# A fused linear-attention and two-MLP kernel: 14 low parts by TensorE and ScalarE, the reciprocals in place, and the last second layers later

## The chip, the cores and the metric

The kernel runs on one core of one Trainium2 chip. The metric is the device time of one execution in microseconds (us), taken as the median of three runs. A profile is one further execution under the hardware profiler; its times count from the first instruction.

## The reference, cut to what matters

Inputs are q, k, v and a decay alpha of shape (4 batches, 8 heads, 768 steps, 48), and weights for two MLPs.

```
state = alpha[t] * state + k[t] v[t]^T          # per batch and head, D = 48
y[t]  = q[t] . state                            # -> x: (3072 tokens, 384)
x1    = elu(x @ w_in) @ w_out                   # hidden 2048
out   = sum over 4 experts e of p[e] * (relu(x1 @ w1[e]) @ w2[e])    # hidden 1024 each
```

## The kernel before

**Attention.** The 768 steps are cut into 6 chunks of 128; a unit is one chunk of one batch (24 units). Within a unit P is the running product of the decay. Scaled by P, q and k turn the recurrence into matrix products: q becomes q*P and k becomes k/P. `prep0` makes P with a VectorE scan and has ScalarE make the reciprocal rP as exp(-ln P). `prep1` (its inner `newton`) refines it on VectorE: t = P*rP, k = k*rP, k = (2 - t)*k. `prep2` makes q = q*P. Then come `scores`, `ktrans` (transposes k through a bank of PSUM), `yout_t` and `state`.

**First MLP.** The float32 operands are split into a high part rounded to float32r and a low part, the rest; a product is three matmuls (high-high, high-low, low-high). An item is one chunk (512 tokens over the 4 batches) with one block of 128 hidden units: 6 x 16 = 96 items. `first` (through `g1`, L422) makes h in a bank of PSUM with 9 matmuls; `elu` is two ScalarE operations (L431, L432) and one VectorE operation in PSUM (L433, the `unit`); `parts` (L438, L439) has ScalarE copy h to the high part g[:,0] and VectorE subtract that from h to give the low part g[:,1]; `second` (through `g2a`, L447) takes both parts two iterations later in 9 matmuls.

**Order.** During this loop TensorE, ScalarE, VectorE and GpSimd each execute strictly in the order in which the code emits their instructions. `self.later` puts an operation into a queue that the next `flush` emits; there are two flushes in an iteration. Each iteration also has two slots, (i, 0) and (i, 1), which carry the steps of the attention units of the next chunk and, in the first 12 iterations, the conversion of the remaining first-MLP weights (`conv_f64`: one ScalarE scaling L406, three VectorE bit operations L77 to L83, then a ScalarE high copy L375 and a VectorE low part L376). The first 14 items (`WIDE`) are "late": the unit is the last thing emitted in the iteration, and the two parts are made in the next one.

**Banks.** `first` and `ktrans` draw their banks from the same ring of three (h0, h1, h2) in turn. A bank is free again when its low part has been made. In chunk 0, `ktrans` falls in slots (0, 0), (3, 0), (6, 1) and (9, 1); after each of them the next two `first` calls are given the bank of the item two before, where otherwise it is that of the item three before.

**Second MLP.** Three rounds of 11 groups; each group has 15 steps (11 in the last one of a round). A step is 3 matmuls (L726) into a bank, then VectorE operations that combine it with running sums (S0 to S5), some on GpSimd. The second-layer matmuls (L773) of the group before are spread between the steps in proportion to a weight per step, `cum`, built from the count of VectorE operations. In group 0 there is no group before; there the second layers of the last two first-MLP items, in six pieces of 3 matmuls (L447), stand between the steps. From group 1 on the ring has two banks.

Of the kernel before, what the change touches and what calls it, by code (L numbers as in the profile page):

```python
# [8 lines left out]
F32 = mybir.dt.float32  # L9
# [78 lines left out]
class _Fast:  # L88
# [50 lines left out]
    def consts(self):  # L139
        nc, const = self.nc, self.const  # L140
        self.zero = self.big.tile([128, 512], mybir.dt.bfloat16, tag="X1", name="zero")
        nc.vector.memset(self.zero, 0.0)
        self.plo = const.tile([128, 1], F32, name="plo")
        nc.vector.memset(self.plo, P_LO)
        self.ident = const.tile([128, 128], F32, name="ident")
        make_identity(nc, self.ident)
        self.mask = const.tile([128, 128], mybir.dt.bfloat16, name="mask")
        nc.gpsimd.memset(self.mask, 1.0)
        nc.gpsimd.affine_select(
            out=self.mask, in_=self.mask, compare_op=ALU.is_ge, fill=0.0,  # L150
            base=0, pattern=[[1, 128]], channel_multiplier=-1,
        )
        self.pacc = const.tile([128, 2 * NCH * B], F32, name="pacc")
        nc.vector.memset(self.pacc, 0.0)
        self.st = []
        for b in range(B):
            s = self.ap.tile([128, NP, 64], F32, tag=f"st{b}", name=f"st{b}")
            nc.vector.memset(s, 0.0)
            self.st.append(s)

    def warm(self, n):
        if n:
# [35 lines left out]
    def prep0(self, u):  # L198


        nc = self.nc
        raw = self.raw[u]
        Pf = self.ap.tile([128, NP * (C + 2)], F32, tag="P", name="P", bufs=3)
        P = Pf.rearrange("p (a t) -> p a t", a=NP)[:, :, 2:C + 2]
        rP = self.ap.tile([128, NP, C], F32, tag="rP", name="rP", bufs=3)
        nc.vector.tensor_tensor_scan(
            Pf, raw[:, A0:V0], self.plo.to_broadcast([128, V0 - A0]), 1.0, ALU.mult, ALU.max
        )
        n = 2 * (u[0] * B + u[1])
        l = self.ap.tile([128, NP, C], F32, tag="rP", name="lnP", bufs=3)  # L210

        def inverse():
            nc.scalar.activation(out=l, in_=P, func=AF.Ln)
            nc.scalar.activation(out=rP, in_=l, func=AF.Exp, scale=-1.0, accum_out=self.pacc[:, n:n + 1])
            nc.scalar.activation(out=l, in_=l, func=AF.Exp, accum_out=self.pacc[:, n + 1:n + 2])

        self.later(inverse)
        self.P[u], self.rP[u] = P, rP

    def prep1(self, u):  # L220

        nc = self.nc
        raw, P, rP = self.raw[u], self.P[u], self.rP.pop(u)
        k = raw[:, K0:A0].rearrange("p (a t) -> p a t", a=NP)

        def newton():
            t = self.ap.tile([128, NP, C], F32, tag="rP", name="nt", bufs=3)
            nc.vector.tensor_tensor(out=t, in0=P, in1=rP, op=ALU.mult)
            nc.vector.tensor_tensor(out=k, in0=k, in1=rP, op=ALU.mult)
            nc.vector.scalar_tensor_tensor(  # L230
                out=k, in0=t, scalar=2.0, in1=k, op0=ALU.subtract, op1=ALU.mult, reverse0=True
            )

        self.later(newton)

    def prep2(self, u):
        nc = self.nc
        raw, P = self.raw[u], self.P[u]
        q = raw[:, Q0:K0].rearrange("p (a t) -> p a t", a=NP)
        nc.vector.tensor_tensor(out=q, in0=q, in1=P, op=ALU.mult)  # L240

    def scores(self, u):

# [134 lines left out]
    def unit_steps(self, u, nxt):  # L378
# [4 lines left out]
        s.append(N(self.prep1))  # L383
        s.append([(self.xtrans, ((u[0], u[1] - 1),))] if u[1] else [])
        s.append([(self.yout_t, (u,))] + ([] if last else [(self.state, (u,))]))
        s.append(N(self.prep2))
        return s


# [431 lines left out]
    def run(self):  # L821
# [26 lines left out]
        def prep(u):  # L848
            self.prep0(u)
            self.prep1(u)  # L850
            self.prep2(u)

        pe_order = tc.manual_schedule(engines={mybir.EngineType.PE})
        pe_order.__enter__()
# [101 lines left out]
        order.__enter__()  # L956
        self.queue = []

        gone = None
        for i in range(n1):  # L960
            h, late = first(items[i]), i < WIDE
            if gone:
                gs[items[i - 1]], low = self.parts(gone)
            self.flush()
            for s in slots.pop((i, 0), []):
                do(s)
            if gone:
                low()
                gone = None
            unit = self.elu(h)  # L970
            if not late:
                unit()
            self.flush()
            if i >= LA:
                second(items[i - LA])
            for s in slots.pop((i, 1), []):
                do(s)
            for f, a in post.pop(i, []):
                f(*a)
            if late:  # L980
                unit()
                gone = h
            else:
                gs[items[i]], low = self.parts(h)
                self.queue.insert(0, low)
# [7 lines left out]
        for i in range(ng + 1):  # L993
# [2 lines left out]
            if i:  # L996
                self.hb = ("h0", "h1")
            if i == 0:
                first_work = {1 + 2 * n: (it, k) for n, (it, k) in enumerate((it, k) for it in items[-LA:] for k in range(KD))}
            elif i > 0:  # L1000
                work = self.layer2(i - 1, G.pop(i - 1))
            if i == ng:
# [23 lines left out]
                    for j in range(1, 5):  # L1026
                        put((2, 5, 8, 9)[j - 1], self.load_xc, r + 1, j)

            dve = [sum(1 for o in ops if "b" in o[2:]) for _, ops in (STEPS if q < NG - 1 else STEPS2)]
            cum = [0]  # L1030
            for n in range(steps):
                cum.append(cum[-1] + 1 + dve[n] + (dve[n - 1] if n else 0))
# [198 lines left out]
```

## Time and profile before

| | |
|---|---|
| median of 3 runs | 1266.61 us (1266.56 to 1269.72) |
| profiled execution: its own time | 1271.87 us |
| its span, first to last instruction | 1270.1 us |
| TensorE matmul busy | 1244.1 us (98%) |
| VectorE, ScalarE, GpSimd busy | 891.5, 588.6, 484.8 us |
| mean granted TensorE clock | 0.990 of full speed |

Busy times are of the profiled execution. Matmuls are pipelined, so a busy TensorE is not necessarily one at its peak. A group's mean duration is longer than the distance between two starts of such instructions in a row, because successive ones overlap.

### The profile page before, as it was taken

What the parts mean: (1) busy time and instruction counts of PE and PEld (TensorE: products, weight loads), DVE (VectorE), ACT (ScalarE), POOL (GpSimd) and SP (SyncE); (2) the same over time, 40 slices, a digit from 0 to 9 for tenths busy, and PEclk for the clock granted to TensorE, in tenths of its full rate; (3) what the DMA queues carried; (4) which work ended last, traced back from release to release, by engine and by line L of the source; (5) the groups of instructions that cost most, each with busy time, mean ns of one, the idle gap of its engine ahead of it and who ended that gap; (6) DMA issues with size and microseconds to landing.
All of it is one profiled execution on the core that took longest, in us unless ns stands there. A gap on an engine that the chain in (4) does not pass through costs nothing.

```text
span 1270.1 us, 17591 instructions
## 1 busy us (share of the span) xinstructions
PE 1244.1 (98%) x6457; PEld 1013.5 (80%) x6457; DVE 891.5 (70%) x1465; ACT 588.6 (46%) x1076; POOL 484.8 (38%) x378
## 2 busy tenths in 40 slices
PE   8899999999999999999999999999999999999997
PEld 5677888888888788878888887888888878888886
DVE  7999677777777758766666756675767575766664
ACT  5666566666656667544343423333343324233241
POOL 0000000000000000066778856777878475356562
PEclk8799999999999999999999999999999999999999
DMA  6564346464756455835464477855456774435231
GB/s 232 180 218 156 105 151 229 178 214 167 251 187 224 159 193 211 281 124 215 160 238 167 170 284 285 304 191 218 164 204 236 276 266 169 158 135 181 100 124 66
DMA packets 71535, 246.80 MB, mean 194 GB/s; under 512 B 6680, under 2 KB 38264, under 8 KB 62096
## 3 DMA queue, kind: packets, MB, share of 16 engines
q1 hardware_dynamic: 70576, 240.87, 53.6%
q10 hardware_dynamic: 864, 4.72, 0.9%
q8 instruction: 53, 0.87, 0.3%
q14 instruction: 42, 0.34, 0.1%
HBM read 182.21 MB, written 63.36 MB: 193 GB/s over the span
## 4 chain that ended last, share of the span: by engine, by line
PE 88%; DVE 7%; issue 2%; ACT 1%; POOL 1%; DMA 0%; DVEq 0%; POOLq 0%; ACTq 0%
PE h L726 25%; PE t L773 14%; PE t L447 14%; PE h L422 13%; PE a L773 10%; PE h L773 5%; PE a L250 1%; PE a L307 1%; PE a L314 1%; DVE cv L80 1%; DVE cv L83 1%; PE h L271 1%; PE a L341 1%; DVE w_W L376 1%; DVE sm L258 1%
## 5 line engine op out<-in xcount | busy, mean ns | idle before, releaser
L704 POOL TENSOR_TENSOR g_W<-c,g_W 128x512 fp32r<-128x512 f32 x128 | 164.5, 1300 | 677.6 <-DVE u L746 538.8
L746 DVE TENSOR_TENSOR u<-h,u 128x512 f32<-128x512 f32 x258 | 177.6, 688 | 86.5 <-PE h L726 85.6
L422 PE MATMUL h<-x,w_W 128*128 128x512 f32 x864 | 218.4, 397 | 8.3 <-DVE g L439 8.2
L726 PE MATMUL h<-xc_Q,wa 128*128 128x512 f32 x780 | 219.0, 390 | 2.7 <-DVE c L746 2.0
L447 PE MATMUL t<-g,w_W 128*128 128x512 f32 x864 | 215.1, 392 | 0.3 <-DVE g L439 0.3
L701 ACT ACTIVATE g_W<-c 128x512 fp32r<-128x512 f32 x128 | 80.2, 627 | 270.1 <-DVE c L746 153.5
L422 PEld LDWEIGHTS h<-x,w_W 128*128 128x128 f32 x864 | 162.3, 190 | 44.8 <-DVE g L439 9.7
L447 PEld LDWEIGHTS t<-g,w_W 128*128 128x128 f32 x864 | 160.9, 188 | 34.6 <-DVE g L439 0.7
L726 PEld LDWEIGHTS h<-xc_Q,wa 128*128 128x128 f32 x780 | 146.0, 188 | 34.8 <-DVE c L746 2.5
L773 PE MATMUL t<-g_W,wb 128*128 128x512 f32 x576 | 157.6, 389 | 0.0
L773 PEld LDWEIGHTS t<-g_W,wb 128*128 128x128 f32 x576 | 108.1, 188 | 22.6
L702 ACT ACTIVATE c<-c 128x512 f32<-128x512 f32 x192 | 121.5, 633 | 7.3
L433 DVE SCALAR_TENSOR_TENSOR h<-e,h 128x512 f32<-128x512 f32 x96 | 66.6, 693 | 73.9 <-ACT e L432 73.8
L746 DVE TENSOR_TENSOR c<-u,h 128x512 f32<-128x512 f32 x123 | 84.1, 686 | 47.4 <-PE h L726 42.7
L740 DVE COPY u<-h 128x512 f32<-128x512 f32 x99 | 67.9, 690 | 64.1 <-PE h L726 62.7
L726 PE MATMUL h<-xc_W,wa 128*128 128x512 f32 x390 | 109.8, 390 | 0.7 <-DVE c L746 0.7
L704 POOL TENSOR_TENSOR g_X<-c,g_X 128x512 fp32r<-128x512 f32 x64 | 82.0, 1297 | 69.3 <-ACT c L702 65.9
L773 PE MATMUL a<-g_W,wb 128*128 128x512 f32 x384 | 108.2, 389 | 0.0
L701 ACT ACTIVATE g_X<-c 128x512 fp32r<-128x512 f32 x64 | 40.1, 627 | 132.0 <-DVE c L746 73.2
L726 PEld LDWEIGHTS h<-xc_W,wa 128*128 128x128 f32 x390 | 72.9, 188 | 17.3 <-DVE c L746 1.6
L431 ACT ACTIVATE e<-h 128x512 f32<-128x512 f32 x96 | 57.3, 597 | 60.8 <-PE h L422 59.4
L439 DVE TENSOR_TENSOR g<-h,g 128x512 fp32r<-128x512 f32 x96 | 65.8, 686 | 26.8 <-ACT g L438 26.5
(138 smaller groups left out, 1861.0 us busy)
## 6 DMA issues: line engine op xcount, KB each, us to landing
wa<-wad SPq DMA_DIRECT2D x33, 1536.0 KB, 6.5
wb<-wbd SPq DMA_DIRECT2D x30, 1536.0 KB, 7.2
raw<-in_att_dram SPq DMA_DIRECT2D x22, 964.0 KB, 5.2
wad<-wh SPq DMA_DIRECT2D x44, 384.0 KB, 2.9
wbd<-wh SPq DMA_DIRECT2D x43, 384.0 KB, 3.7
xcd<-xh SPq DMA_DIRECT2D x30, 512.0 KB, 2.9
wraw<-in_wm_dram SPq DMA_DIRECT2D x16, 768.0 KB, 4.3
wraw<-in_we_dram SPq DMA_DIRECT2D x20, 576.0 KB, 4.7
```

The lines of the kernel that those rows point to most:

```text
L422: nc.tensor.matmul(h[:, 0:n], w[:, wl, fi, k * 128:(k + 1) * 128], x[:, xl, k, n0:n0 + n], start=(k == 0 and i == 0), stop=(k == KD - 1 an ...
L431: nc.scalar.activation(out=e, in_=h, func=AF.Relu, scale=-1.0)
L433: return lambda: nc.vector.scalar_tensor_tensor(out=h, in0=e, scalar=-1.0, in1=h, op0=ALU.add, op1=ALU.max)
L439: return g, lambda: nc.vector.tensor_tensor(out=g[:, 1], in0=h, in1=g[:, 0].bitcast(F32), op=ALU.subtract)
L447: nc.tensor.matmul(self.xa[k][:, 0:n], w[:, wl, fi, DM + k * 128:DM + (k + 1) * 128], g[:, gl, 0:n], start=(first and i == 0), stop=(last ...
L701: nc.scalar.activation(out=g[:, n, 0], in_=v, func=AF.Relu)
L702: nc.scalar.activation(out=v, in_=v, func=AF.Relu)
L704: lambda: nc.gpsimd.tensor_tensor(out=g[:, n, 1], in0=v, in1=g[:, n, 0].bitcast(F32), op=ALU.subtract)
L726: nc.tensor.matmul(b, w[:, wl], x[:, xl], start=(j == 0), stop=(j == 2))
L740: nc.vector.tensor_copy(out, b)
L746: (nc.vector if "b" in (a0, a1) or dst == "S5" else nc.gpsimd).tensor_tensor(out=out, in0=val(a0, b), in1=val(a1, b), op=ALU.add if op == ...
L773: nc.tensor.matmul(oa[m, d], wt[:, f, wl, d * 128:(d + 1) * 128], G[m][:, f, gl], start=first, stop=last)
```

## The change

1. For the first 14 items the VectorE subtraction L439 goes. In its place TensorE adds -1 times the high part to h in its bank (one matmul with a new tile `minus`, minus the identity), emitted after `second`, and ScalarE copies the bank to g[:,1], emitted after slot (i, 1) and what follows it.
2. rP is written over the decay values in the unit's raw tile. `newton` now multiplies q and rP by P in one VectorE operation of 2 x 512 columns; `prep2` goes, and with it the separate tile for rP and t.
3. The six pieces of the last two second layers in group 0 move from after steps 1, 3, 5, 7, 9, 11 to after steps 4, 7, 9, 11, 13, 14.
4. The weight of a step counts the VectorE operation on S5 that reads no bank (one, in step 7 of every group but the last of a round).

```diff
+        self.minus = self.ap.tile([128, 128], F32R, tag="minus", name="minus")
+        nc.scalar.mul(self.minus, self.ident, -1.0)
...
-        rP = self.ap.tile([128, NP, C], F32, tag="rP", name="rP", bufs=3)
+        rP = raw[:, A0:A0 + NP * C].rearrange("p (a t) -> p a t", a=NP)
...
-        l = self.ap.tile([128, NP, C], F32, tag="rP", name="lnP", bufs=3)
+        l = self.ap.tile([128, NP, C], F32, tag="lnP", name="lnP", bufs=2)
...
         def newton():
-            t = self.ap.tile([128, NP, C], F32, tag="rP", name="nt", bufs=3)
-            nc.vector.tensor_tensor(out=t, in0=P, in1=rP, op=ALU.mult)
             nc.vector.tensor_tensor(out=k, in0=k, in1=rP, op=ALU.mult)
+            qr = raw[:, 0:3 * NP * C].rearrange("p (x a t) -> p x a t", x=3, a=NP)[:, 0:3:2]
+            nc.vector.tensor_tensor(
+                out=qr, in0=qr, in1=P.unsqueeze(1).to_broadcast([128, 2, NP, C]), op=ALU.mult
+            )
             nc.vector.scalar_tensor_tensor(
-                out=k, in0=t, scalar=2.0, in1=k, op0=ALU.subtract, op1=ALU.mult, reverse0=True
+                out=k, in0=rP, scalar=2.0, in1=k, op0=ALU.subtract, op1=ALU.mult, reverse0=True
             )
...
-        s.append(N(self.prep2))
+        s.append([])
...
             if gone:
-                gs[items[i - 1]], low = self.parts(gone)
+                g, _ = self.parts(gone)
+                gs[items[i - 1]] = g
             self.flush()
             for s in slots.pop((i, 0), []):
                 do(s)
-            if gone:
-                low()
-                gone = None
             unit = self.elu(h)
...
             if i >= LA:
                 second(items[i - LA])
+            if gone:
+                nc.tensor.matmul(gone, self.minus, g[:, 0], start=False, stop=True, skip_group_check=True)
             for s in slots.pop((i, 1), []):
                 do(s)
             for f, a in post.pop(i, []):
                 f(*a)
+            if gone:
+                nc.scalar.copy(g[:, 1], gone)
+                gone = None
             if late:
                 unit()
                 gone = h
...
-                first_work = {1 + 2 * n: (it, k) for n, (it, k) in enumerate((it, k) for it in items[-LA:] for k in range(KD))}
+                pieces = [(it, k) for it in items[-LA:] for k in range(KD)]
+                first_work = dict(zip((4, 7, 9, 11, 13, 14), pieces))
...
-            dve = [sum(1 for o in ops if "b" in o[2:]) for _, ops in (STEPS if q < NG - 1 else STEPS2)]
+            dve = [sum(1 for o in ops if "b" in o[2:] or o[1] == "S5") for _, ops in (STEPS if q < NG - 1 else STEPS2)]
```

## Rows read from the trace of the kernel before

**Rows 1.** The page: busy tenths and granted TensorE clock, 40 slices of 31.75 us

```profile
DVE  7999677777777758766666756675767575766664
...
PEclk8799999999999999999999999999999999999999
```

**Rows 2.** Stages by window: start:end, length, then busy us (instructions) per engine, clock

```profile
44.00:127.69 83.69, 74.63 (x500) 58.72 (x499) 80.62 (x117) 54.90 (x95) 0.00 (x0) 0.94 0.56 187
127.69:532.08 404.39, 404.31 (x2495) 330.26 (x2496) 296.81 (x574) 257.29 (x520) 0.00 (x0) 1.00 0.57 196
```

**Rows 3.** Waits of TensorE, 40 to 135 us: total, times, longest

```profile
PE h L422 <- DVE g L439: 8.2, 3, 4.2
PE a L250 <- ACT cv L406: 0.5, 1, 0.5
```

**Rows 4.** Timeline of TensorE, first layer: start, length, instruction [idle before]

```profile
54.70 4.21 PE L422 MATMUL h<-x,w_W 128*128 128x512 f32 x9 [4.19 <-DVE g L439]
...
63.91 2.20 PE L422 MATMUL h<-x,w_W 128*128 128x512 f32 x9
...
69.68 2.20 PE L422 MATMUL h<-x,w_W 128*128 128x512 f32 x9
...
73.78 2.33 PE L422 MATMUL h<-x,w_W 128*128 128x512 f32 x9
...
86.49 2.33 PE L422 MATMUL h<-x,w_W 128*128 128x512 f32 x9
...
93.34 3.79 PE L422 MATMUL h<-x,w_W 128*128 128x512 f32 x9 [2.47 <-DVE g L439]
...
113.94 2.33 PE L422 MATMUL h<-x,w_W 128*128 128x512 f32 x9 [1.54 <-DVE g L439]
...
120.73 2.34 PE L422 MATMUL h<-x,w_W 128*128 128x512 f32 x9
...
133.72 2.20 PE L422 MATMUL h<-x,w_W 128*128 128x512 f32 x9
```

**Rows 5.** Timeline of VectorE in iterations 1 and 2

```profile
53.96 0.68 DVE L439 TENSOR_TENSOR g<-h,g 128x512 fp32r<-128x512 f32 x1
54.56 0.68 DVE L228 TENSOR_TENSOR nt<-P,rP 128x512 f32<-128x512 f32 x1
...
61.88 0.35 DVE L351 TENSOR_TENSOR tmp<-a,st 128x192 f32<-128x192 f32 x1
```

**Rows 6.** Timeline of ScalarE: iterations 1, 4 and 7

```profile
56.03 0.92 ACT L406 ACTIVATE cv<-wraw 128x768 f32<-128x768 f32 x1
...
70.72 0.59 ACT L438 CAST g<-h 128x512 fp32r<-128x512 f32 x1 [1.51 <-DVE h L433]
...
75.93 0.50 ACT L375 CAST x<-xr 128x384 fp32r<-128x384 f32 x1
...
92.73 0.63 ACT L213 ACTIVATE lnP<-P 128x512 f32<-128x512 f32 x1 [1.82 <-DVE P L206]
...
94.78 0.89 ACT L406 ACTIVATE cv<-wraw 128x768 f32<-128x768 f32 x1
```

**Rows 7.** Groups by line and shape: busy us, mean ns, idle before

```profile
L439 DVE TENSOR_TENSOR g<-h,g 128x512 fp32r<-128x512 f32 x96 | 65.8, 686 | 26.8 <-ACT g L438 26.5
...
L438 ACT CAST g<-h 128x512 fp32r<-128x512 f32 x96 | 56.2, 586 | 47.8 <-DVE h L433 47.3
...
L376 DVE TENSOR_TENSOR w_W<-cv,w_W 128x768 fp32r<-128x768 f32 x16 | 15.2, 950 | 0.0
```

**Rows 8.** Timelines of TensorE and VectorE where group 0 ends

```profile
548.56 0.96 PE L726 MATMUL h<-xc_Q,wa 128*128 128x512 f32 x3 [2.04 <-DVE c L746]
...
547.81 0.69 DVE L746 TENSOR_TENSOR c<-u,h 128x512 f32<-128x512 f32 x1
```

**Rows 9.** Waits of TensorE, 566 to 1260 us

```profile
PE h L726 <- DVE c L746: 0.7, 2, 0.4
PE h L726 <- DVE u L746: 0.7, 2, 0.4
```

More of the change, by code (lines that the diff above doesn't have):

```diff
@@ L226, in newton @@
         def newton():
-            t = self.ap.tile([128, NP, C], F32, tag="rP", name="nt", bufs=3)
-            nc.vector.tensor_tensor(out=t, in0=P, in1=rP, op=ALU.mult)
             nc.vector.tensor_tensor(out=k, in0=k, in1=rP, op=ALU.mult)
+            qr = raw[:, 0:3 * NP * C].rearrange("p (x a t) -> p x a t", x=3, a=NP)[:, 0:3:2]
+            nc.vector.tensor_tensor(
+                out=qr, in0=qr, in1=P.unsqueeze(1).to_broadcast([128, 2, NP, C]), op=ALU.mult
+            )
             nc.vector.scalar_tensor_tensor(
-                out=k, in0=t, scalar=2.0, in1=k, op0=ALU.subtract, op1=ALU.mult, reverse0=True
+                out=k, in0=rP, scalar=2.0, in1=k, op0=ALU.subtract, op1=ALU.mult, reverse0=True
             )
         self.later(newton)
[L236 to L240, printed above, removed]
     def scores(self, u):
@@ L850, in prep @@
             self.prep1(u)
-            self.prep2(u)
         pe_order = tc.manual_schedule(engines={mybir.EngineType.PE})
```

## The prediction

> **What bounds the kernel now.** The tenths of the page come first: VectorE stands at 9 from the second to the fourth slice and the granted clock is below full there; later neither holds [rows 1]. The windows put edges to it. From 44.0 us, where the first item starts, to 127.7 us VectorE is busy 80.6 of 83.7 us and TensorE 74.6; from 127.7 to 532.1 us TensorE is busy 404.3 of 404.4 at full clock [rows 2]. So whatever the change does to the attention steps or to the first layer after 127.7 us is worth nothing unless it shortens TensorE, and it doesn't. The question is when TensorE reaches the steady stage: `first(15)`, the first-layer matmuls of item 15, at 133.72 us [rows 4]. The waits then name the limit before that: 8.2 us in three waits of `first` for the VectorE low part g [rows 3], at items 2, 8 and 11 [rows 4]. These are just places where `ktrans` has taken a bank of the ring, so that `first(i)` is given the bank of item i-2: the wait is for a bank, and a bank is free when its low part is made.
>
> **1, the low parts: what goes.** VectorE loses 14 operations. One lasts 0.686 us [rows 7], but the next starts 0.60 us after it [rows 5], so 14 x 0.60 = 8.4 us go from an engine that is nearly full.
>
> **What is added.** TensorE gets 14 matmuls of 512 columns; nine last 2.20 us [rows 4], so 0.24 each, 3.4 us. ScalarE gets 14 copies like L438, 0.59 us [rows 7], 8.3 us on an engine busy 54.9 of 83.7 [rows 2]; in sum that hurts nobody.
>
> **Where the bank is freed.** Here I choose against the sum of loads. Before, VectorE made the low part in mid-iteration. Now the bank needs: high part (ScalarE), then all of `second`, the negative matmul, then whatever ScalarE has before the copy, which is emitted last. All engines keep their order, so I step through the bank's seven gates (`first` of items 2, 4, 5, 7, 8, 10, 11), and take each stretch between gates from the old rows plus 0.24 us for each negative matmul in it. Seven is found from the ring: after each `ktrans` the next two `first` take the bank of item i-2.
>
> *Item 2.* In iteration 1 ScalarE runs the weight scaling L406 at 56.03 us for 0.92 [rows 6]; the low copy comes behind it. With 0.1 us of overlap it ends at 56.85 + 0.59 = 57.44, and `first(2)` starts at 57.5 instead of 54.70 [rows 4]: +2.8. Before, the low part was made at 53.96 [rows 5]. VectorE cannot use its free time: its decay operation needs `state`, which TensorE issues after `first(2)`; it ran at 61.88 [rows 5], and moves with it.
>
> *Items 3, 4.* 63.91 - 54.70 = 9.21 us from `first(2)` to `first(3)`, half clock included [rows 4], plus 0.24: 66.95 (+3.0). To `first(4)` 5.77 plus 0.24, and now a gate: matmul tail and two handovers (0.25, estimated from the 0.06 between the end of the low part and a waiting `first`, twice or so, and a tail) and the copy, 0.59: 73.8 against 69.68, +4.1.
>
> *Item 5.* The low copy of item 2 also stands ahead of item 3's high part on ScalarE, which so moves from 70.72 to about 73.55. From there to the end of the x cast before, 75.93 + 0.50, ScalarE had 5.7 us of work [rows 6]: weights, the logarithm and two exponentials, elu, L406, x. Behind that comes the copy of item 3: 73.55 + 5.7 + 0.5 = 79.8, so `first(5)` moves from 73.78 to 79.8, +6.0.
>
> *Item 7.* 86.49 - 73.78 = 12.71 without an idle TensorE, plus 0.48: 93.0, +6.5. Its own gate is covered by `scores` and `ktrans`, which follow the negative matmul; the same for item 10.
>
> *Item 8.* ScalarE in iteration 7: 2.2 us for `first(7)`, 1.2 for elu, then logarithm and exponentials, 94.78 - 92.73 = 2.05 [rows 6], L406 0.8, copy and handover 0.65: 93.0 + 6.9 = 99.9 against 93.34, +6.5. TensorE has ended `second(5)` and the negative matmul at about 97.45 and idles 2.45 us.
>
> *To the end.* From `first(8)` to `first(12)` it was 120.73 - 93.34 = 27.39 us; less 1.6 of slow clock, 1.54 and 0.45 of idle time [rows 3, 4], plus four negative matmuls (0.96) and 2.4 us of idle at item 11, where the order is that of item 8: 27.2, so 127.1 (+6.4). Three more matmuls (0.7) against the 0.6 us that TensorE loses there now: `first(15)` at 140.2, +6.4 to 6.5. I take +6.4.
>
> **The clock.** After 4.19 and 2.47 us idle the nine matmuls took 4.21 and 3.79 us, half clock for most of them; after 1.54 us idle 2.33 us, full clock [rows 4]. The new idles at items 8 and 11 (2.4 us) are nearest to the one that fell, yet a little shorter: bounds 0 and 2 x 1.6 us. I take one of the two: +1.5.
>
> **A rule that bears on it.** In iteration 7 the L406 at 94.78 needs only weights, yet it runs behind a logarithm that waited 1.82 us for VectorE [rows 6]: ScalarE didn't overtake. The Trainium skill, "PSUM — Partial Sum Buffer", section on engine and sequencer instructions, says the queues of ScalarE, VectorE and GpSimd are strict FIFO; by that rule, with which the trace agrees, the copy waits for the logarithm and the sum stands; if ScalarE could overtake, the copy of item 6 would end some 2 us sooner.
>
> **2, the reciprocals.** `newton` before: three operations of 0.60, plus q 0.60. After: 0.60 + 0.60, and one of 1,024 columns. From 512 to 768 columns the length grows from 0.686 to 0.950 us [rows 7], 1.03 ns a column, so its start-to-start time is 0.60 + 512 x 1.03 ns = 1.13. It saves 0.07 us for each of 24 units, four of which lie in the VectorE stage: 0.3 us, which the gates above swallow. In the prelude it costs or gives 0.6 at most: q*P used to run while VectorE waited for the first exponential, and now comes after it. I take 0 with bounds -0.6 and +0.6. `minus` is one 128-column ScalarE operation under 0.59 us while ScalarE has nothing to do: 0; if it stands ahead of the first logarithm, that is in the 0.6.
>
> **3, the last second layers.** At the end of group 0 TensorE waits 2.04 us for the last VectorE operation, 547.81 + 0.69 [rows 8]. Steps 12 to 14 now have two pieces (2 x 0.68) among them, but steps 0 to 4 are bare: VectorE's seven operations there (4.2 us) outlast five steps of 0.68 us, and step 4 waits about 0.6 for its bank. The same VectorE work, with less waiting in it, ends near 547.7: -0.75, bounds -1.4 and +0.5. The three copies of x1 and their DMA, on ScalarE's queue, move behind the last activations of the group; the banks they free are wanted 10 us later, and the data a round later.
>
> **4, the weights.** TensorE waits 0.7 us behind u and 0.7 behind c in all of the second MLP [rows 9]. More matmuls behind the S5 operation can take the first: -0.7, bounds -1.4 and +0.5 (another step is left shorter).
>
> **The sum.** +6.4 + 1.5 - 0.75 - 0.7 = +6.45 us. The profiled execution took 1271.87 us (span 1270.1 and 1.8 around it), 5.3 above the median; with one profile I carry the difference over: 1266.6 + 6.4 = 1273.0.
>
> **Rivals.**
> *The freed VectorE decides (faster).* If the low copies were done by the time TensorE wants the banks, VectorE's 8.4 us would count; TensorE has 9 us idle and 3.6 of slow clock to give, less 3.4 of new matmuls, so it could follow. 1266.6 - 8.4 - 1.45 = 1257. For it: VectorE is the fuller engine [rows 2]. Against: a negative matmul that waits for `second`. It decides from where the copies end about 0.6 us after the high part, as on VectorE, at items 4, 5 and 8. Chance 0.14.
> *The clock stays up (no change).* The negative matmul of item 0 at about 52.3 us breaks the idle before `first(2)`. If that alone kept full clock, 2.0 us come back, and with no fall at items 8 and 11 the sum is 6.4 - 2.0 - 1.45 = +2.95, less up to 0.6 in the prelude: 1269. Against: over 5 us of idle remain. Chance 0.22.
> *Both new idles halve the clock:* +1.6, 1274.6, within the forecast's range.
>
> **Chances and range.** The forecast has 0.64, with a range of its own of 1269.5 to 1277.5 (clock both ways, prelude, parts 3 and 4 at their bounds). About 0.3% (3.8 us) is what can be told from no change: above 1270.4 lie 0.61 of all, from 1262.8 to 1270.4 0.25 (the clock's rival and the forecast's low end), below 0.14. Down to 1264.5 it takes in the clock's rival and leaves out the faster one.
>
> **What the profile after would show.** Right: waits of `first` for ScalarE's g copy, at items 2, 4, 5, 8 and 11; `first(5)` 5 to 7 us later; VectorE with idle time between 60 and 127 us; `first(15)` near 140; the wait at the end of group 0 under 1.4 us. Wrong: VectorE still without gaps there and `first(15)` before 130, or ScalarE's low copies right behind the high ones.

## The result, and the profile after

The changed kernel is slower: a median of 1278.88 us (1278.56 to 1282.81, 4 runs) against 1266.70 us (1266.56 to 1269.72) for the kernel before, a ratio of 1.0085 with an interval of 1.0065 to 1.0106 (the quotient of these two medians alone is 1.0096). The sign and the place were as predicted. The time lies 5.9 us above the 1273.0 us of the forecast and 1.4 us above the top of its range.

In the profile after, line numbers have moved a little: `first` is L420, `second` L445, the negative matmul L973, the low copy L979, the high copy L436, the weight scaling L404, the scores L248, a step of the second MLP L724 and its combining operations L744. The profiled execution took 1278.56 us, its span is 1276.9 us.

The page comes first: tenths of VectorE and granted clock, in 40 slices of 31.92 us.

```profile
DVE  8788577787777768766667756676767575767664
...
PEclk9799999999999999999999999999999999999999
```

VectorE was at 9 in the second to fourth slice before [rows 1]; it is at 7 or 8 now. So VectorE was freed; the clock is still at 7 in the second slice. The waits of TensorE from 38 to 145 us say what took its place (total us, times, longest):

```profile
PE h L420 <- ACT g L979: 11.5, 5, 4.7
PE h L973 <- ACT g L436: 1.1, 1, 1.1
```

Before, three waits of `first` for VectorE's low part cost 8.2 us [rows 3]; now five waits for ScalarE's low copy cost 11.5. The timeline of TensorE, `first` alone, has them one by one (start, length, instruction, idle time before it and what ended it):

```profile
43.70 2.70 PE L420 MATMUL h<-x,w_W 128*128 128x512 f32 x9
...
56.41 4.21 PE L420 MATMUL h<-x,w_W 128*128 128x512 f32 x9 [4.68 <-ACT g L979]
66.12 2.22 PE L420 MATMUL h<-x,w_W 128*128 128x512 f32 x9
72.99 2.33 PE L420 MATMUL h<-x,w_W 128*128 128x512 f32 x9 [0.68 <-ACT g L979]
79.08 2.34 PE L420 MATMUL h<-x,w_W 128*128 128x512 f32 x9 [1.47 <-ACT g L979]
...
92.18 2.33 PE L420 MATMUL h<-x,w_W 128*128 128x512 f32 x9
99.14 3.88 PE L420 MATMUL h<-x,w_W 128*128 128x512 f32 x9 [2.36 <-ACT g L979]
...
120.79 2.33 PE L420 MATMUL h<-x,w_W 128*128 128x512 f32 x9 [2.36 <-ACT g L979]
...
140.94 2.22 PE L420 MATMUL h<-x,w_W 128*128 128x512 f32 x9
```

They are items 0, 2, 3, 4, 5, 7, 8, 11 and 15: the gates are at items 2, 4, 5, 8 and 11, and `first(15)` starts at 140.94. After each of the two gaps of 2.36 us the nine matmuls could have been slow; they were at item 8 (3.88 us) and not at item 11 (2.33 us).

The span can now be put together from its stretches. Beside the profiled execution of before stands a second one, of experiment e3; all numbers are starts and differences of TensorE rows, in us.

| stretch | before, profiled | before, e3 | after |
|---|---|---|---|
| start to `first(0)` | 44.06 | 39.66 | 43.70 |
| `first(0)` to `first(15)` | 89.66 | 90.31 | 97.24 |
| `first(15)` to the second MLP | 398.36 | 398.23 | 398.22 |
| its group 0 | 16.48 | 16.48 | 15.94 |
| the rest | 721.54 | 721.52 | 721.80 |
| span | 1270.1 | 1266.2 | 1276.9 |

Two things are to be read here. The stage of the items became 6.9 to 7.6 us longer. And the part before `first(0)`, which the prediction put at no change, is 4 us longer than in e3 but not longer than in the profiled execution of before. The median of these four runs (1266.7) is that of an execution like e3 (1267.89), not of the one that was profiled (1271.87). Repeated runs of the kernel before lie mostly around two times, about 1267 and about 1271.5 us, and each of the two profiles is of one of these; the two profiles differ in how much of the time before `first(0)` ran at half clock. The 77 further runs of the kernel before that stand beside the experiments have medians of 1269.2 to 1269.5 us, between the two times; against these the change costs some 9.5 us, not 12.2.

### The profile page after: what moved, and what is told of

Its sections match the earlier page's. It is cut to its first block, busy times and chain, and to the rows that moved or that the text cites. A ratio compares the mean times of both kernels' runs of the same rounds, so it can differ in the third digit from the quotient of the medians.

```text
span 1276.9 us, 17604 instructions
## 1 busy us (share of the span) xinstructions
PE 1243.3 (97%) x6467; PEld 1014.9 (79%) x6471; DVE 883.6 (69%) x1427; ACT 597.4 (47%) x1091; POOL 485.4 (38%) x378
## 4 chain that ended last, share of the span: by engine, by line
PE 92%; ACT 2%; DVE 2%; issue 2%; POOL 1%; DMA 1%; SPq 0%; DVEq 0%; POOLq 0%
PE h L724 24%; PE h L420 15%; PE t L445 15%; PE t L771 14%; PE a L771 10%; PE h L771 5%; PE a L248 2%; PE a L305 2%; PE a L312 2%; PE h L269 1%; PE a L339 1%; PE t L286 1%; POOL acc L793 0%; PE h L167 0%; DMA x0d<-yt 0%
## 5 line engine op out<-in xcount | busy, mean ns | idle before, releaser
L744 DVE TENSOR_TENSOR u<-h,u 128x512 f32<-128x512 f32 x258 | 177.5, 688 | 86.2 <-PE h L724 84.9
L420 PE MATMUL h<-x,w_W 128*128 128x512 f32 x864 | 218.7, 398 | 11.8 <-ACT g L979 11.5
L724 PE MATMUL h<-xc_Q,wa 128*128 128x512 f32 x780 | 219.1, 390 | 0.8 <-DVE c L744 0.7
L445 PE MATMUL t<-g,w_W 128*128 128x512 f32 x864 | 214.8, 392 | 0.0
L420 PEld LDWEIGHTS h<-x,w_W 128*128 128x128 f32 x864 | 162.3, 190 | 48.6 <-ACT g L979 13.6
L445 PEld LDWEIGHTS t<-g,w_W 128*128 128x128 f32 x864 | 160.9, 188 | 34.0 <-issue 0.4
L724 PEld LDWEIGHTS h<-xc_Q,wa 128*128 128x128 f32 x780 | 145.8, 188 | 33.1 <-DVE u L744 1.7
L744 DVE TENSOR_TENSOR c<-u,h 128x512 f32<-128x512 f32 x123 | 84.3, 686 | 48.5 <-PE h L724 43.0
L724 PE MATMUL h<-xc_W,wa 128*128 128x512 f32 x390 | 109.6, 390 | 2.2 <-DVE u L744 2.2
L724 PEld LDWEIGHTS h<-xc_W,wa 128*128 128x128 f32 x390 | 73.0, 188 | 18.2 <-DVE u L744 3.2
L771 PEld LDWEIGHTS a<-g_W,wb 128*128 128x128 f32 x384 | 72.1, 188 | 15.0
```

The costliest lines, as they stand in the source:

```text
L420: nc.tensor.matmul(h[:, 0:n], w[:, wl, fi, k * 128:(k + 1) * 128], x[:, xl, k, n0:n0 + n], start=(k == 0 and i == 0), stop=(k == KD - 1 an ...
L445: nc.tensor.matmul(self.xa[k][:, 0:n], w[:, wl, fi, DM + k * 128:DM + (k + 1) * 128], g[:, gl, 0:n], start=(first and i == 0), stop=(last ...
L724: nc.tensor.matmul(b, w[:, wl], x[:, xl], start=(j == 0), stop=(j == 2))
L744: (nc.vector if "b" in (a0, a1) or dst == "S5" else nc.gpsimd).tensor_tensor(out=out, in0=val(a0, b), in1=val(a1, b), op=ALU.add if op == ...
L771: nc.tensor.matmul(oa[m, d], wt[:, f, wl, d * 128:(d + 1) * 128], G[m][:, f, gl], start=first, stop=last)
```

## The experiments

Each run has its own kernels before beside it on the same chip; their medians were 1269.49, 1269.24 and 1269.37 us (19 to 31 runs each).

**e1 to e4: the parts apart.** e1 is the kernel before with part 1 alone, e2 the changed kernel without part 1, e3 the kernel before again, without an edit, and e4 the changed kernel with part 1 moved up: the negative matmul ahead of `second`, the low copy right behind `elu`'s two ScalarE operations.

```diff
# e1, against before
+        self.minus = ...
-                gs[items[i - 1]], low = self.parts(gone)
+                g, _ = self.parts(gone)
+                gs[items[i - 1]] = g
-            if gone:
-                low()
-                gone = None
...
+            if gone:
+                nc.tensor.matmul(gone, self.minus, g[:, 0], start=False, stop=True, skip_group_check=True)
...
+            if gone:
+                nc.scalar.copy(g[:, 1], gone)
+                gone = None
# e2, against after: these lines back as they were before
# e4, against after
+            if gone:
+                nc.tensor.matmul(gone, self.minus, g[:, 0], start=False, stop=True, skip_group_check=True)
             unit = self.elu(h)
+            if gone:
+                nc.scalar.copy(g[:, 1], gone)
+                gone = None
...
             if i >= LA:
                 second(items[i - LA])
-            if gone:
-                nc.tensor.matmul(gone, self.minus, g[:, 0], start=False, stop=True, skip_group_check=True)
...
-            if gone:
-                nc.scalar.copy(g[:, 1], gone)
-                gone = None
```

> The kernel before with part 1 alone (low parts of 14 items by TensorE and ScalarE). Theory G (the bank of an item is freed late, because the low copy stands behind second, the negative matmul and ScalarE's other work): nearly all of the loss, 1274 to 1280 us, first of items 2, 4, 5, 8 and 11 waiting for ScalarE's low copy, first(15) near 140 us. Rival P (the reciprocals in place, through another order in the prelude, or the phase of the clock they bring): 1265 to 1269 us.

> The changed kernel with the low parts back on VectorE, parts 2 to 4 kept. Theory G: 1264 to 1268 us, waits of first for VectorE's low part at items 2, 8 and 11 as in the kernel before. Rival P: 1274 us or more.

> The kernel before, unchanged, to have a trace of another execution: the profiled one took 1271.9 us where the median is 1266.7. Theory C (the 5 us are the clock: fewer matmuls at half clock around the waits of first at items 2 and 8): in an execution of 1266 to 1267 us first(2) and first(8) take about 2.2 us instead of 4.2 and 3.8, and the granted clock is above 0.990. Rival: the same clock, and the 5 us lie in the prelude or in the second MLP.

> The changed kernel with the negative matmul ahead of second and the low copy right behind elu's two ScalarE operations, ahead of logarithms, weights and slot work. Theory G: the low part is ready about 2 us after first, before second has ended, so no first waits for it; VectorE's 8.4 us then count: 1257 to 1264 us. Rival L (14 more matmuls and 14 more ScalarE copies cost what was lost, wherever they stand): 1274 us or more.

| | ratio to before | start to `first(0)` | to `first(15)` |
|---|---|---|---|
| e1, part 1 only | 1.0075 (1.0051 to 1.0098) | 38.91 | 95.09 |
| e2, without part 1 | 1.0030 (1.0015 to 1.0044) | 43.58 | 90.13 |
| e3, before again | 0.9992 (0.9974 to 1.0010) | 39.66 | 90.31 |
| e4, part 1 early | 1.0035 (1.0017 to 1.0053) | 48.63 | 90.48 |

The waits of TensorE from 38 to 145 us in e1, where L424 is `first`, L983 the low copy and L440 the high copy:

```profile
PE h L424 <- ACT g L983: 11.5, 5, 4.7
PE h L977 <- ACT g L440: 1.8, 1, 1.8
```

and in e4, where L970 is the low copy and L967 the negative matmul:

```profile
PE h L420 <- ACT g L970: 4.1, 2, 3.2
PE h L967 <- ACT g L436: 3.4, 3, 1.5
```

By their times only e1 came as its theory had it (a median of 1278.79 us). e2 (1274.26) and e4 (1274.95) missed theirs and ended at the figures of their rivals, and in e3 the rival held: items 2 and 8 took 4.21 and 3.47 us again, and what it is shorter by lies ahead of `first(0)`. The stages say more than the times.

Part 1 alone brings the same five waits and the longer stage. Without it, or with its copy early, the stage is as long as before (90.1 and 90.5 against 89.7 and 90.3). That shows where the 7 us come from: not from the work itself, which e4 has too, but from where in the order the bank is freed (two of the five waits are left in e4, 3.15 us at item 2 and 0.95 at item 5). e4 says a second thing. Its VectorE is as free as in the changed kernel, and the time still isn't under that of before. The windows of e4's stage (length, then busy us and instructions of TensorE, its weight loads, VectorE, ScalarE and GpSimd, then clock, DMA share and GB/s):

```profile
48.63:139.11 90.48, 82.91 (x539) 64.85 (x539) 74.68 (x101) 64.98 (x116) 0.00 (x0) 0.96 0.52 174
```

VectorE fell from 80.6 of 83.7 us [rows 2] to 74.7 of 90.5, but TensorE is busy 82.9 us and idles for 7.5, which the two waits above fill (4.1 and 3.4). The wait for the bank has become a wait for the high part plus a matmul.

And e2, which has nothing of part 1, is still 0.3% above before. That was the first sign that something else costs time; its stage is not longer, its time before `first(0)` is, beside e3's.

The fastest executions are compared as a check on additivity: 1266.56 of before, 1273.98 of e1 (+7.4), 1271.01 of e2 (+4.5); the sum, 11.9, is what the changed kernel has over before (1278.56, +12.0). At the medians it doesn't add up: e1 is 9.3 and e2 4.8 us above the kernels before that stand beside them, and the changed kernel 9.5 us above those same runs; e1's median is already that of the changed kernel (1278.79 and 1278.88). e1's other five runs lie up to 7 us higher, at granted clocks from 0.993 to 0.986, where the fastest had 0.994; only the fastest was profiled, so where they lose it isn't shown.

**e5: what stands ahead of the copy on ScalarE.** Against after, the copy alone moves, ahead of slot (i, 1).

```diff
                 nc.tensor.matmul(gone, self.minus, g[:, 0], start=False, stop=True, skip_group_check=True)
+                nc.scalar.copy(g[:, 1], gone)
+                gone = None
             for s in slots.pop((i, 1), []):
                 do(s)
...
-            if gone:
-                nc.scalar.copy(g[:, 1], gone)
-                gone = None
```

> The changed kernel with one edit: ScalarE's low copy stands right behind the negative matmul, ahead of slot (i, 1), so that the weight scaling and the x cast no longer precede it; second still does. Theory G: first of items 2, 5, 8 and 11 each 0.8 to 1.2 us earlier after its gate, the stage from first(0) to first(15) 92 to 95 us instead of 97.2. Rival L (the load of the added operations): 97 us still.

The ratio is 1.0105 (1.0073 to 1.0137), the stage 95.21 us. The timeline of TensorE in e5, items 2, 8 and 11:

```profile
55.83 3.82 PE L420 MATMUL h<-x,w_W 128*128 128x512 f32 x9 [3.90 <-ACT g L974]
...
98.23 2.33 PE L420 MATMUL h<-x,w_W 128*128 128x512 f32 x9 [3.02 <-ACT g L974]
...
118.93 2.35 PE L420 MATMUL h<-x,w_W 128*128 128x512 f32 x9 [3.00 <-ACT g L974]
```

Item 2's wait fell from 4.68 to 3.90 us; those of items 8 and 11 rose from 2.36 to about 3.0. Of the 2.03 us between the stages of after and e5, 1.55 are item 8 at full clock and 0.39 item 2's matmuls (3.82 us for 4.21); the five waits grew in sum from 11.5 to 12.2 us. So moving the copy ahead of the slot's work gained nothing, and of the 0.8 to 1.2 us that were expected at each of four items only item 2 shows some (0.78 us). Why is in ScalarE's timeline, iterations 6 and 7 of e5:

```profile
89.21 0.59 ACT L974 CAST g<-h 128x512 fp32r<-128x512 f32 x1 [0.58 <-PE h L973]
89.69 0.92 ACT L404 ACTIVATE cv<-wraw 128x768 f32<-128x768 f32 x1
...
95.57 0.63 ACT L215 ACTIVATE lnP<-P 128x512 f32<-128x512 f32 x1 [1.34 <-DVE P L208]
...
97.62 0.57 ACT L974 CAST g<-h 128x512 fp32r<-128x512 f32 x1
```

The copy of iteration 6 now waits for the negative matmul, and the weight scaling L404 behind it starts no sooner than in after (89.69 and 89.67), although `first(7)` is 1.57 us earlier. VectorE's operations on that weight and the scan behind them so keep their old times too (the scan starts at 94.31, in after at 94.25). The logarithm, which comes with a flush ahead of the next copy, waits 1.34 us for that scan, and its two exponentials follow. Of the places tried only the one ahead of the flush and of `second`, in e4, shortened the stage beyond the clock. e4 moves the matmul and the copy at once; what each of the two is worth wasn't taken apart.

**e6 to e8: the time before `first(0)`.** e6 is before with part 2 alone. e7 is e6 with 18 matmuls on zeros ahead of the scores of the fourth unit. e8 is the changed kernel, in which the units before item 0 make rP*P and q*P in two operations.

```diff
# e6, against before: part 2 of the change and nothing else
# e7, against e6
+            if i == 3:
+                self.warm(18)
             if i < B:
                 self.scores(w)
# e8, against after, in newton
+            if self.queue is None:
+                nc.vector.tensor_tensor(out=rP, in0=rP, in1=P, op=ALU.mult)
+                nc.vector.scalar_tensor_tensor(
+                    out=k, in0=rP, scalar=2.0, in1=k, op0=ALU.subtract, op1=ALU.mult, reverse0=True
+                )
+                return
# and behind prep1
+            nc.vector.tensor_tensor(out=q, in0=q, in1=self.P[u], op=ALU.mult)
```

> The kernel before with part 2 alone (reciprocals in place, q and reciprocal in one operation). Theory K (a single idle of TensorE of some 4 us before the scores of the fourth unit, after which the matmuls of 32 to 40 us run at half clock in nearly all executions): first(0) at 43 us or later, 1270 to 1276 us. Rival: the loss without part 1 is made by parts 3 and 4, and this one spreads as the kernel before does, 1266.7 to 1271.8 us.

> Part 2 alone, with 18 warm-up matmuls on zeros ahead of the scores of the fourth unit, where TensorE idled. They give nothing but activity. Theory K: the clock stays full between 30 and 40 us, first(0) near 39.5 to 41 us, 1266 to 1269 us in most executions. Rival (VectorE's longer operation itself delays the prelude): first(0) still at 43 us or later.

> The changed kernel, but in the prelude q and the reciprocal are multiplied by P in two operations again, q's in its old place. Theory K: some executions have the fast prelude (first(0) near 39.7 us) and end at 1272 to 1275 us, the median is 1 to 5 us below that of the changed kernel. Rival: 1278 to 1283 us as the changed kernel.

| | ratio to before | start to `first(0)` |
|---|---|---|
| e6, part 2 only | 1.0044 (1.0028 to 1.0059) | 47.65 |
| e7, e6 with warm matmuls | 1.0050 (1.0036 to 1.0065) | 42.20 |
| e8, after with the operation split | 1.0079 (1.0050 to 1.0109) | 46.88 |

Part 2 alone costs 0.44%, with a median of 1276.11 us, just above the 1270 to 1276 that were expected. e7 and e8 missed: e7's median is 1275.25 us where 1266 to 1269 were expected, and none of e8's four runs was below 1277.39. Over all profiles with before's own operations there and no more warm matmuls (before, e1, e3, e9, e11) `first(0)` starts at 38.9 to 44.1 us, with part 2 and no warm matmuls (after, e2, e4, e5, e6, e8) at 43.6 to 48.6. The place can be seen in the order of VectorE. The operations of one unit in e3, where the scores can start (28.51 to 29.98), and the TensorE rows that follow:

```profile
28.51 0.68 DVE L228 TENSOR_TENSOR nt<-P,rP 128x512 f32<-128x512 f32 x1
29.11 0.69 DVE L229 TENSOR_TENSOR raw<-raw,rP 128x512 f32<-128x512 f32 x1
29.71 0.35 DVE L353 TENSOR_TENSOR st<-a,P 128x192 f32<-128x192 f32 x1
29.98 0.68 DVE L230 SCALAR_TENSOR_TENSOR raw<-nt,raw 128x512 f32<-128x512 f32 x1
```

```profile
30.77 0.34 PE L250 MATMUL t<-raw 48*128 48x128 f32 x1 [0.35 <-PE t L288]
...
39.66 2.70 PE L422 MATMUL h<-x,w_W 128*128 128x512 f32 x9
```

The same unit after, on VectorE (L229 is k*rP, L231 the doubled operation, L208 the scan of another unit, L234 the last of k), and on TensorE:

```profile
28.74 0.69 DVE L229 TENSOR_TENSOR raw<-raw 128x512 f32<-128x512 f32 x1
29.34 0.56 DVE L77 TENSOR_SCALAR cv<-cv 128x768 int32<-128x768 int32 x1
29.81 1.22 DVE L231 TENSOR_TENSOR raw<-raw,P 128x1024 f32<-128x1024 f32 x1
30.95 1.24 DVE L208 TENSOR_TENSOR_SCAN P<-raw,plo 128x520 f32<-128x520 f32 x1
32.10 0.67 DVE L234 SCALAR_TENSOR_TENSOR raw<-raw 128x512 f32<-128x512 f32 x1
```

```profile
32.87 0.55 PE L248 MATMUL t<-raw 48*128 48x128 f32 x1 [4.30 <-issue]
```

k is ready at 32.77 us rather than at 30.66, because a weight conversion, the doubled operation and another unit's scan run between its two operations. TensorE idles 4.30 us in one piece (the trace names no releaser, but k's operation ends 0.10 us before), and it works on at a lower clock: 0.63 and 0.69 in the windows of after from 30 to 35 and 35 to 40 us, 1.00 in both in e3. From the scores to `first(0)` it then takes 10.83 us instead of 8.89. The 4.04 us between after and e3 are thus 2.10 of later scores and 1.94 of slower work behind them. A long gap isn't the only way to the lower clock, though: the profiled execution of before had 0.74 and 0.58 in these windows, and from 20 us to `first(0)` no gap of TensorE in it is longer than 0.78 us.

e7 parts these two. Its warm matmuls fill the gap, and the timeline of TensorE shows the gap still ended by k's operation (L232 in e7):

```profile
28.19 4.05 PE L165 MATMUL h<-zero 128*128 128x512 bf16 x18
32.60 0.37 PE L246 MATMUL t<-raw 48*128 48x128 f32 x1 [0.36 <-DVE raw L232]
```

From the scores to `first(0)` it now takes 9.60 us, where e6 took 12.03 and after 10.83: the clock is back, at 1.00 in both windows. Yet `first(0)`, at 42.20, is still 2.5 us later than in e3: the scores start 1.83 us later, and 0.71 us more pass behind them at full clock. Of after's 1.94 us some 1.2 are thus the clock. And e7's median didn't fall: the profiled execution (1272.10 us, mean clock 0.995) is one of its fastest, and five of its ten runs have a mean clock of 0.988 or 0.989, close to most of e6's. Where those lose it wasn't profiled.

e8 shows that the length of the doubled operation isn't the whole cause. With two operations of 512 columns the gap was still 3.22 us:

```profile
35.33 0.55 PE L254 MATMUL t<-raw 48*128 48x128 f32 x1 [3.22 <-issue]
```

No scan stands between the two operations on k there, but two low parts and the multiplication of rP do (31.94 to 34.54 us).

**e9: before's operations put back there.** Against after: own tiles for rP, lnP and t, `nt` and q*P as before for the units before item 0, the new form within the items; part 1 as in e4; part 4 undone.

```diff
+        if self.queue is None:
+            rP = self.ap.tile([128, NP, C], F32, tag="rP", name="rP", bufs=3)
+        else:
             rP = raw[:, A0:A0 + NP * C].rearrange("p (a t) -> p a t", a=NP)
-        l = self.ap.tile([128, NP, C], F32, tag="lnP", name="lnP", bufs=2)
+        l = self.ap.tile([128, NP, C], F32, tag="rP", name="lnP", bufs=3)
...
+            if self.queue is None:
+                t = self.ap.tile([128, NP, C], F32, tag="rP", name="nt", bufs=3)
...
+                return
...
-            dve = [sum(1 for o in ops if "b" in o[2:] or o[1] == "S5") ...
+            dve = [sum(1 for o in ops if "b" in o[2:]) ...
```

> The changed kernel with the prelude's reciprocals as before (own tiles, four operations), the early negative matmul and low copy of the run e4, and without part 4; part 2 stays in the item loop, part 3 stays. Theory G and K together: first(0) at 38.5 to 40 or near 44 us as in the kernel before, first(0) to first(15) 88.5 to 91 us, 1264.5 to 1271 us. Rival (the loss of part 2 comes from the item loop, or from what the fourth run shared with it): first(0) to first(15) over 91 us, 1272 us or more.

The ratio is 1.0013 (0.9996 to 1.0031), the median 1271.11 us and the stage 91.38 us, both just above what was expected. The gap before the scores is 0.35 us, as in e3, and `first(0)` starts at 41.82 (the clock was 0.50 from 15 to 20 us):

```profile
32.88 0.34 PE L259 MATMUL t<-raw 48*128 48x128 f32 x1 [0.35 <-PE t L297]
```

So the tiles and the independent operations together are what had kept the order short. Which of the two does (writing rP over the decay, the chain in place, or one buffer less) wasn't taken apart.

**e10 to e12: can anything be won?** e10 is e9 with 9 more warm matmuls at the start and 13 on zeros ahead of `first(2)`; e12 is before with 9 and 17 of them; e11 is before with part 1 only for the seven items whose bank isn't asked for early (1, 4, 7, 10 to 13).

```diff
# e10 (13) against e9, e12 (17) against before
-        self.warm(18)
+        self.warm(27)
...
+            if i == 1:
+                wb = self.bank("t0")
+                for _ in range(13):
+                    nc.tensor.matmul(wb, self.zero[:, 0:128], self.zero, start=True, stop=True)
# e11, against before: part 1 under this condition
+                by_pe = i - 1 in (1, 4, 7, 10, 11, 12, 13)
...
-            if gone:
+            if gone and not by_pe:
                 low()
                 gone = None
```

> The run e9 with matmuls on zeros added where TensorE idles: 9 more at the very start and 13 in iteration 1 ahead of first(2). Theory C (a good part of the idle time's price is the clock): granted clock full through the first 40 us and first(2) in 2.3 instead of 4.2 us; 2 to 5 us below e9, 1261 to 1266 us. Rival (the clock falls at other places then, in the small matmuls of the attention): as e9.

> The kernel before with part 1 for items 1, 4, 7 and 10 to 13 only, those whose bank is asked for three items later or has work to hide behind; the low parts of the other seven stay on VectorE. Theory G: no first waits for a ScalarE low copy and the 7 operations freed on VectorE shorten the waits at items 8 and 11, first(0) to first(15) 86 to 90 us. Rival L (each operation moved costs): half of the loss of part 1, 92 to 94 us.

> The kernel before with 9 more warm-up matmuls at the start and 17 matmuls on zeros in iteration 1 ahead of first(2), where TensorE idled 4.2 to 4.5 us. Theory C: first(2) at full clock, 2.3 instead of 4.2 us, and the slow prelude (first(0) at 44 us) rarer: median 2 to 5 us below the kernel before. Rival: no difference.

The ratios are 0.9997 (0.9978 to 1.0017), 1.0000 (0.9985 to 1.0015) and 1.0000 (0.9984 to 1.0016): none beats the kernel before, where 2 to 5 us were expected of e10 and e12. e10 ran at full clock up to `first(15)` (item 2 in 2.34 us, a stage of 88.99 us), and its fastest run, 1266.33 us, is no faster than the fastest of before, 1266.15. e12 shows why the clock alone isn't worth much. Its timeline of TensorE, items 2, 5 and 10:

```profile
50.48 2.37 PE L422 MATMUL h<-x,w_W 128*128 128x512 f32 x9 [0.49 <-DVE g L439]
...
69.56 3.78 PE L422 MATMUL h<-x,w_W 128*128 128x512 f32 x9 [2.11 <-DVE g L439]
...
104.34 3.84 PE L422 MATMUL h<-x,w_W 128*128 128x512 f32 x9
```

Item 2 took 2.37 us where it had taken 4.21 [rows 4], and idle time came back elsewhere: 2.11 us ahead of item 5 and 2.0 us ahead of the scores before item 10, and both items ran slow. The stage was 90.14 us, between the 89.66 and 90.31 of before. VectorE is busy for 85.1 us of it, which fits VectorE as the limit; no run shows it more directly. In e11 it loses 7 of its operations, and the waits of `first` for the low part stay at the same three items (7.3 us in sum, 8.2 before [rows 3]); the stage, 88.58 us, is within what was expected, but item 8 at full clock alone (2.35 us for 3.79) is more than the 1.08 us by which it is shorter than in the profiled before.

## Why the prediction was right in sign and short in size

**The gates of part 1: right.** The five waits are at the five items named, and `first(5)` is 5.3 us later, `first(15)` at 140.94 for 140.2 plus the clock's 1.5. Counted from `first(0)`, which moved by -0.36 us, items 2, 4, 5, 7 and 8 are later by 2.1, 3.7, 5.7, 6.1 and 6.2 us; 2.8, 4.1, 6.0, 6.5 and 6.5 were worked out. The stage grew by 7.58 us; without the 1.55 that item 8 lost to the clock the gates cost 6.0 (6.4 predicted). Both are net of the 1.5 us or so that item 8 had lost to the clock in before too (3.79 us [rows 4]). e1, which has no slow item but item 2, agrees: 95.09, with 0.56 for its shorter item 2, is 6.0 above 89.66. ScalarE's timeline in iteration 7 of after shows the term that carried the sum, the copy behind the logarithm and the weight scaling:

```profile
95.71 0.62 ACT L215 ACTIVATE lnP<-P 128x512 f32<-128x512 f32 x1
...
97.75 0.87 ACT L404 ACTIVATE cv<-wraw 128x768 f32<-128x768 f32 x1
98.52 0.57 ACT L979 CAST g<-h 128x512 fp32r<-128x512 f32 x1
98.98 0.60 ACT L436 CAST g<-h 128x512 fp32r<-128x512 f32 x1
```

The negative matmul was done 1.73 us before the copy started at 98.52. The distance was 1.73 us at item 11 too, 4.06 at item 2 and 0.84 at item 5: there ScalarE's order is the limit. Only at item 4 did the copy wait for the negative matmul (0.91 us), which stands behind `second`. At item 8 the copy waits in ScalarE's own queue. The Trainium skill, "PSUM — Partial Sum Buffer", section "Engine vs sequencer instructions", calls ScalarE's queue strict FIFO; this trace agrees, and in e5 the order of the code alone moved the copy ahead of L404 and left it behind L215.

**The clock: right, by the value taken between the bounds.** One of items 8 and 11 was halved (+1.55; +1.5 predicted). Which one, and whether any, differs between executions: in e1 and e8 neither was, nor in e5 after longer gaps. That the profile of after shows just the one that was taken is luck.

**VectorE idle, and the wait that VectorE now has: right.** From 59.42 + 0.95 to 63.83 us it has nothing to do, because its decay operation follows `first(2)`:

```profile
59.42 0.95 DVE L374 TENSOR_TENSOR w_W<-cv,w_W 128x768 fp32r<-128x768 f32 x1
63.83 0.36 DVE L349 TENSOR_TENSOR tmp<-a,st 128x192 f32<-128x192 f32 x1 [3.46 <-PE a L339]
```

**Part 2: the step that failed.** "In the prelude it costs or gives 0.6 at most ... I take 0." It cost 4.0 us beside e3 (after 43.70 and e2 43.58 against 39.66), nothing beside the profiled execution of before (44.06), and 0.44% by itself over ten runs (e6). The step counted operations and their lengths, and took their order for given. Ahead of item 0 the order isn't that of the code: in after, another unit's scan runs between two operations of this unit. Part 2 changed that order, k came 2.1 us later, and the clock was lower behind the gap. A bound for this edit should have had the next operation of each kind on VectorE in it (a scan, 1.2 us, a conversion, 0.9) and the half clock behind a longer gap, some 4 us, not 0.6. How much of the miss this step makes isn't settled: e1, without part 2, has the median of the changed kernel.

**Carrying the difference over: failed too, and hid the first.** The prediction took 5.3 us off the profiled execution and carried the rest over. Profile against profile the change made 1278.56 - 1271.87 = 6.7 us, for 6.45 predicted. But the profiled execution of before was one that had lost time ahead of `first(0)` (clock 0.53 and 0.78 from 15 to 25 us, 0.74 and 0.58 from 30 to 40), and an execution like e3 had lost less there (0.66 from 15 to 20 us alone). The 5.3 us weren't an offset common to all executions; they lay in the same stretch that part 2 makes longer. After showed no such better level: none of its four runs was below 1278.56, none of e8's four below 1277.39. That profile against profile came out so near is in this part luck: the profiled before had lost to the clock what part 2 costs. And the three runs that gave 1266.6 were low themselves. From the 1269.4 of the later runs the same +6.4 leads to 1275.8, which is 3.1 us short in place of 5.9.

**Part 3: right, a little oversized.** Group 0 takes 15.94 us instead of 16.48, -0.54 for -0.75. The rows of TensorE and VectorE where it ends show a wait of 0.68 where 2.04 us stood [rows 8]:

```profile
555.10 0.96 PE L724 MATMUL h<-xc_Q,wa 128*128 128x512 f32 x3 [0.68 <-DVE c L744]
```

```profile
554.36 0.69 DVE L744 TENSOR_TENSOR c<-u,h 128x512 f32<-128x512 f32 x1
```

The shorter wait has a second worth, which the prediction left out. In the seven profiles that keep the wait of 2.04 us the granted clock of the 6 us behind it is 0.72 in three (e1, e7, e11) and 1.00 in four (before, e3, e6, e12); in the seven with 0.68 us it is 1.00. The fall costs 1.6 us. In e1's timeline of TensorE three matmuls there take 1.46 and the next four 1.91 us, where e3 has 0.85 and 1.07:

```profile
548.79 0.96 PE L728 MATMUL h<-xc_Q,wa 128*128 128x512 f32 x3 [2.04 <-DVE c L748]
...
550.06 1.46 PE L728 MATMUL h<-xc_Q,wa 128*128 128x512 f32 x3
551.31 1.91 PE L775 MATMUL a<-g_W,wb 128*128 128x512 f32 x4
```

**Part 4: wrong in sign, small.** The waits of TensorE from 560 to 1260 us:

```profile
PE h L724 <- DVE u L744: 2.2, 2, 1.1
```

The 0.7 behind c [rows 9] is gone, as said, but the 0.7 behind u became 2.2: +0.8 in sum for -0.7. "Another step is left shorter" was written as the bound of +0.5, and that is the one that came, beyond its bound in the waits; the stretch after group 0 is 0.3 us longer. e1 and e9, without part 4, keep c at 0.8 and u at 0.7.

**The rivals.** "The freed VectorE decides" fell: e4 removes its late copies, and VectorE's freed time still gives nothing, since 14 matmuls and the waits for the high parts fill TensorE's gaps. "The clock stays up" fell at item 2: the nine matmuls took 4.21 us again, with the negative matmul ahead of the gap.

**Still open:** which of the edits in part 2 changes VectorE's order; where the slower executions of e1 and e7 lose their time; and a part of the stretch after `first(15)`, which was longer in e1 and e7 (1138.3 and 1139.0 us against 1136): 1.6 us are the fall of the clock after group 0, the other 0.4 and 1.2 us weren't traced.

## What to carry to other kernels

Moving work to an emptier engine is worth what its result's time is worth: ask when it gives the shared buffer back, behind what it stands on the new engine, and who asks for that buffer next. An edit of operations or of their tiles can reorder a stretch whose order isn't written by hand, so its price there is not the sum of its lengths but the longer operations that may come between, and the idle time behind them. When the profiled execution isn't at the median, find out first in which stretch it differs; if the change touches that stretch, the difference can't be carried over. A few runs of a kernel with two levels of time are not a base to add to.

## What the runs showed of the hardware

The granted clock isn't set by the length of a gap alone. The same wait of 2.04 us at the same place was followed by a fall in three profiles and by none in four. Nine matmuls ran slow after gaps of 1.97 us (e2, item 11, 3.92 us), 2.11 (e12) and 2.36 (after, item 8), and at full clock after 2.36 (after, item 11), 3.02 and 3.00 us (e5) and 3.50 us (e2, item 2, 2.34 us). The Trainium skill, "TensorE: Matmul & The Clock Gate", Part 1, says that the number of slow matmuls at the start of one kernel varies from run to run. The runs here agree for the time before `first(0)` (a granted clock of 0.53 in one execution of the kernel before and 0.66 in another, from 15 to 20 us), and show the same in mid-kernel, where even two equal gaps in one execution differ.

An operation of VectorE on 1,024 columns lasts 1.22 us and the next starts 1.14 us after it, within 0.01 of the 1.13 worked out from 512 and 768 columns: merging two of 512 (0.60 each from start to start) saves 0.06 us.
